# Lightning attention and a gated feed-forward on one core: another order of the work on Pool, Vector and TensorE

## The chip, the cores and the metric

The kernel runs on one core of one Trainium2 chip. The metric is the time of one execution on the device in microseconds (us); four runs of the kernel before gave a median of 242.67 us (241.29 to 244.12). The core's engines are TensorE (PE in the profile; its weight loads are PEld), Vector (DVE), Scalar (ACT), Pool (GpSimd) and Sync (SP). Each takes its own instructions strictly in the order in which the program issues them. Transfers are issued by Pool or by Sync and then carried out by 16 DMA engines.

## The reference

Two stages. The first is linear attention with a decay per head, over batch 4, 8 heads, 768 positions and a head width of 64. The second is a feed-forward with a sigmoid gate on 3072 tokens of width 512, hidden width 1536.

```python
# attention, block by block; lam is one decay per head
intra = einsum('bhic,bhjc->bhij', qb, kb) * Dmask      # Dmask: lam ** (i - j), lower triangle
intra = einsum('bhij,bhjd->bhid', intra, vb)
inter = einsum('bhid,bhde->bhie', qb * lam_pow, kv_state)
out[:, :, sl] = intra + inter
kv_state = lam_block * kv_state + einsum('bhsd,bhse->bhde', kb * rev_pow, vb)
# feed-forward, x is the attention's output with the heads side by side
gate = 1 / (1 + exp(-(x @ w_gate)))
out = (gate * (x @ w_val)) @ w_out
```

## The kernel before

**Tiling.** The kernel uses blocks of 128 positions in place of the reference's 64, so there are six steps n = 0 to 5. In each step it handles 4 batches x 128 positions = 512 tokens. Inputs are cast from float32 to bfloat16 by the loads; products are summed in float32 in PSUM, of which attention has five banks (pool ps_at) and the feed-forward three (ps_ff).

**Pieces.** The work of a step is cut into pieces, each a few lines of code:

- t(n, bp), piece_t: the transposed q of two batches is scaled by the powers of the decay into QS, on Vector (L177, for n > 1, from the tile QR). For n = 0 and 1 TensorE transposes q and k (L160, L169, L184, L190); from n = 2 on transpose_by_dma (L151) makes QR and KR by two transposing transfers on Sync's queue.
- sc(n, bp), m(n, bp): scores of two batches on TensorE (piece_s, L206, two banks for a batch), then the mask product MT, two Vector operations for each batch (piece_m, L214). sc issues the scores of both batches and the masks of the first, m those of the second.
- a(n, bp), piece_a: attention output of two batches on TensorE, from the state Sb (L220) and from MT and v (L227); Scalar copies it to XT (L234), the feed-forward's input.
- make_kd(n): the decayed k, kd, one operation on Pool over 128 x 2048 elements (L238). fade(): the decayed state sd, one Pool operation for each batch (L247).
- c(n, bp), piece_c: the state's update, kd times v on TensorE (L255), added to sd on Vector and written to Sb (L264; for n = 0 a copy, L262).
- gv(n, ft), piece_gv: four gate matmuls (L275), a sigmoid on Scalar (L278), four value matmuls (L281), and on Vector the product ht (L284). Twelve of these make a step. gvh is the same for two batches only (L292 to L302).
- po(n, tt), piece_po: one batch's output projection, twelve matmuls (L307), copied by Scalar (L310) and sent out on Sync's queue (L311).
- load(n, what, b0, b1), L78: q, k or v of a block, issued by Pool. load_gv and load_wo (L84, L85, L89): a slice of the weights, issued by Pool.
- idle(n): matmuls on zeros that keep TensorE busy while block 0 waits for data (L140).

**Order.** Nothing plans the order: it is written by hand, under manual_schedule, and every engine follows the order of the calls. Block 0 (L328 to L351) goes through transposes, scores, masks and attention with idle() between. Pool has by then issued block 0's loads and three slices of weights; make_kd(0), the other slices and the loads of block 1 stand behind them (L314 to L326). Then come the twelve gv of step 0 with the attention of block 1 among them, step 1 with block 1's second half, and from L412 the eight output projections of steps 0 and 1 with block 2's attention between them. The loop from L429 handles steps 2 to 5: in step n, the state's update c(n) after the first two gv, the load of block n + 2, fade and make_kd(n + 2) on Pool, then t, sc, m and a of block n + 1 among gv 2 to 11, and at the end four po in a row. The load of a block and its transposes are issued a step ahead.

Of the kernel before, what the change touches and what calls it, by code (L numbers as in the profile page):

```python
# [8 lines left out]
FP32 = mybir.dt.float32  # L9
# [7 lines left out]
def kernel(  # L17
# [14 lines left out]
    C = 128  # L32
# [49 lines left out]
    def load_gv(i, w):  # L82
        fs = slice(i * w, (i + 1) * w)
        nc.gpsimd.dma_start(out=WG[:, :, fs], in_=wg_r[:, :, fs])  # L84
        nc.gpsimd.dma_start(out=WV[:, :, fs], in_=wv_r[:, :, fs])  # L85
# [12 lines left out]
    nc.vector.memset(ident, 0.0)  # L98
    nc.vector.memset(tri, 0.0)

    load(0, "q", 0, 2)
    load(0, "k", 0, 2)
    for i, base in enumerate((-1, C - 1)):
# [6 lines left out]
                            pattern=[[-1, C]], channel_multiplier=1)  # L110
    load(0, "q", 2, 4)
    load(0, "k", 2, 4)
    load(0, "v", 0, 2)
    load(0, "v", 2, 4)

# [20 lines left out]

    def idle(n, cols=TCH):
        w = ps_ff.tile([128, TCH], FP32, name="wm", tag="ff")
        for i in range(n):
            nc.tensor.matmul(w[:, :cols], lhsT=zero[:, :128], rhs=zero[:, :cols], start=True, stop=True,  # L140
                             skip_group_check=True)
# [13 lines left out]

    def piece_tq0(bp):
        tq = ps_at.tile([128, 2, HP, C], BF16, name="tq", tag="ps")
        for i in range(2):
            for hp in range(HP):
                nc.tensor.transpose(tq[:, i, hp, :], Q[0][:, 2 * bp + i, 2 * hp:2 * hp + 2, :], ident)  # L160
        QS[0, bp] = trsb.tile([128, 2, HP, C], BF16, tag="QS", name="QS")
        nc.vector.tensor_tensor(out=QS[0, bp], in0=tq,
                                in1=lamq.unsqueeze(1).to_broadcast([128, 2, HP, C]), op=ALU.mult)

# [28 lines left out]

    Sb = stp.tile([128, B, HP, 128], BF16, tag="Sb", name="Sb")

    SP, OP = {}, {}

    def piece_s(n, bs):

        for b in bs:  # L200
            bp, i = b // 2, b % 2
            sp = [ps_at.tile([128, HP, C], FP32, name=f"sp{u}", tag="ps") for u in range(2)]
            for hp in range(HP):
                for u in range(2):
                    us = slice(u * 64, (u + 1) * 64)
                    nc.tensor.matmul(sp[u][:, hp, :], lhsT=KS[n, bp][us, i, hp, :],  # L206
                                     rhs=QS[n, bp][us, i, hp, :],
                                     start=(hp == 0), stop=(hp == HP - 1), skip_group_check=True)
            SP[n, b] = sp

    def piece_m(n, b):
# [4 lines left out]
    def piece_a(n, bs):  # L216
# [16 lines left out]
        for b in bs:  # L233
            nc.scalar.copy(XT[n][:, :, b, :], OP[n, b])  # L234

    def make_kd(n):
# [77 lines left out]
    GW = DFF // 6  # L314
    for i in range(3):
        load_gv(i, GW)
    make_kd(0)
# [7 lines left out]
    for i in range(3):  # L325
        load_wo(i, NFT // 3)  # L326

    idle(10)  # L328
    piece_tq0(0)
    idle(4)  # L330
    piece_tk0(0)
    idle(2)
    piece_s(0, [0])
    piece_m(0, 0)
    piece_tq0(1)
    piece_s(0, [1])
    piece_m(0, 1)
    idle(3)
    piece_tk0(1)
    idle(2)  # L340
    piece_s(0, [2])
    piece_m(0, 2)
    piece_s(0, [3])
    piece_m(0, 3)
    nc.vector.memset(Sb, 0.0)
    piece_a(0, [0])
    piece_a(0, [1])
    idle(2)
    piece_a(0, [2])
    piece_a(0, [3])  # L350
    idle(2)  # L351

    def c(n, bp):
        piece_c(n, [2 * bp, 2 * bp + 1])
# [14 lines left out]
    def gv(n, *fts):  # L369
        for ft in fts:  # L370
            piece_gv(n, ft)
# [21 lines left out]
    load(2, "qkv", 0, B)  # L393
    make_kd(2)
    transpose_by_dma(2)
# [7 lines left out]
    gvh(1, 1, 0, 1, 2, 3, 4, 5, 6)  # L403
    gv(1, 7, 8)
    c(1, 0)
    gv(1, 9)
    c(1, 1)
    load(3, "qkv", 0, B)
    fade()
    make_kd(3)  # L410
    gv(1, 10, 11)
    piece_po(0, 0)  # L412
    t(2, 0)
    piece_po(0, 1)
    sc(2, 0)
    m(2, 0)
    t(2, 1)
    piece_po(0, 2)
    sc(2, 1)
    m(2, 1)  # L420
    piece_po(0, 3)
    transpose_by_dma(3)
    piece_po(1, 0)
    a(2, 0)
    piece_po(1, 1)
    a(2, 1)
    piece_po(1, 2)
    piece_po(1, 3)
    for n in range(2, NSTEP):  # L429
        nx = n + 1  # L430
        if nx < NSTEP:
            gv(n, 0)
            c(n, 0)
            gv(n, 1)
            c(n, 1)
            if n + 2 < NSTEP:
                load(n + 2, "qkv", 0, B)
                fade()
                make_kd(n + 2)
            elif nx < NSTEP - 1:  # L440
                fade()
            gv(n, 2)
            t(nx, 0)
            gv(n, 3)
            t(nx, 1)
            gv(n, 4)
            sc(nx, 0)
            gv(n, 5)
            m(nx, 0)
            gv(n, 6, 7)  # L450
            sc(nx, 1)
            gv(n, 8)
            m(nx, 1)
            if n + 2 < NSTEP:
                transpose_by_dma(n + 2)
            a(nx, 0)
            gv(n, 9, 10, 11)
            a(nx, 1)
        else:
            gv(n, *range(NFT))  # L460
        for tt in range(B):
            piece_po(n, tt)

# [29 lines left out]
```

## Time and profile before

| | |
|---|---|
| median of four runs | 242.67 us |
| the profiled execution | 242.25 us |
| its span | 240.1 us |
| TensorE busy | 224.4 us (93%) |
| Vector busy | 114.6 us (48%) |
| Pool busy | 85.6 us (36%) |
| Scalar busy | 80.1 us (33%) |
| mean granted TensorE clock | 0.989 |

The profile shows one execution. Its span runs from the first to the last instruction; the time of the same execution is 2.15 us longer. In a row of the timeline stand the start in us from the span's start, the length, the engine, the line of the kernel, the operation, what it writes <- what it reads, and in brackets the time for which the engine stood before it and what ended that. In a row of the waits stand the waiting engine, its line, what it waited for, then the total in us, how often, and the longest. A row of the windows gives the stretch, its length, and for each engine its busy time and instructions, then the granted clock. A row of the transfers ends with their size and the us from issue to landing; a row of one line's instructions gives the shortest, the median and the longest in ns. A busy time of TensorE holds overlaps, so the length from one start to another is the better measure of what it costs.

### The profile page before, as it was taken

The page shows a single profiled execution, that of the slowest core. Times are in us where ns is not written, and L with a number is a line of the kernel's source. Part 1 is how long each engine was busy: PE and PEld are TensorE (multiplying, and loading weights), DVE is VectorE, ACT ScalarE, POOL GpSimd, SP SyncE. Part 2 cuts the span into 40 slices and gives each one's busy share as a digit, 9 for nine tenths or more (in the row PEclk, how much of TensorE's full clock was granted, in tenths as well). Part 3 has the DMA queues.
Part 4 walks back from the last instruction along what each step waited for, and adds up shares of the span by engine and source line. Part 5 has one row for each costly group of instructions (what it writes and reads, how often), then busy time and mean ns, then how long its engine had stood idle before and what let it go on. Part 6 is the DMA issues. An engine that isn't in the chain of part 4 may idle for free.

```text
span 240.1 us, 3816 instructions
## 1 busy us (share of the span) xinstructions
PE 224.4 (93%) x1528; PEld 115.8 (48%) x1553; DVE 114.6 (48%) x184; ACT 80.1 (33%) x145; POOL 85.6 (36%) x70
## 2 busy tenths in 40 slices
PE   7779999999995999988999997999999999999993
PEld 2444555886542454544554543554544554444441
DVE  2473845744839400799510599620497510243300
ACT  5453244453211033322431332432222431323121
POOL 8999676924976700497000390000000000000000
PEclk9999999999999799999999999999999999999998
DMA  8999999999999999979923750002200002100022
GB/s 54 149 184 194 174 183 168 208 157 155 148 157 221 97 179 146 266 153 98 156 11 130 157 67 0 0 3 87 87 3 1 0 3 99 75 0 0 3 87 87
DMA packets 102289, 24.89 MB, mean 104 GB/s; under 512 B 91520, under 2 KB 99200, under 8 KB 102272
## 3 DMA queue, kind: packets, MB, share of 16 engines
q0 software_dynamic: 82032, 14.16, 80.7%
q1 hardware_dynamic: 20240, 10.49, 20.5%
q8 instruction: 12, 0.20, 0.3%
q14 instruction: 5, 0.04, 0.0%
HBM read 28.32 MB, written 6.29 MB: 144 GB/s over the span
## 4 chain that ended last, share of the span: by engine, by line
PE 87%; DVE 4%; DMA 3%; issue 2%; POOL 2%; ACT 1%; POOLq 0%; DVEq 0%
PE po L307 25%; PE gp L275 24%; PE vp L281 23%; PE sp L206 3%; DMA kb<-in_k_dram 3%; PE vp L298 3%; PE op L227 3%; PE gp L292 2%; PE cp L255 2%; PE op L220 2%; DVE MT L214 2%; DVE QS L177 1%; POOL qb L78 1%; DVE ht L284 1%; POOL kb L78 0%
## 5 line engine op out<-in xcount | busy, mean ns | idle before, releaser
L284 DVE TENSOR_TENSOR ht<-sg,vp 128x512 bf16<-128x512 bf16 x65 | 44.6, 686 | 91.9 <-PE vp L281 90.5
L275 PE MATMUL gp<-XT,WG 128*128 128x512 bf16 x249 | 65.2, 379 | 3.4 <-DVE ht L284 2.4
L281 PE MATMUL vp<-XT,WV 128*128 128x512 bf16 x255 | 66.0, 379 | 0.3
L307 PE MATMUL po<-WO,ht 128*128 128x512 bf16 x281 | 64.2, 383 | 0.4
L278 ACT ACTIVATE sg<-gp 128x512 bf16<-128x512 f32 x65 | 38.8, 597 | 76.4 <-PE gp L275 72.5
L307 PEld LDWEIGHTS <-ht 128*128 128x128 bf16 x288 | 27.9, 99 | 33.7 <-issue 1.3
L281 PEld LDWEIGHTS <-WV 128*128 128x128 bf16 x260 | 25.4, 98 | 30.7
L275 PEld LDWEIGHTS <-WG 128*128 128x128 bf16 x260 | 24.1, 98 | 29.6 <-issue 3.8
L214 DVE TENSOR_TENSOR MT<-sp,mask 128x512 bf16<-128x512 f32 x48 | 30.5, 682 | 7.6 <-PE sp L206 7.6
L310 ACT COPY ob<-po 128x512 f32<-128x512 f32 x24 | 14.1, 586 | 55.0 <-PE po L307 51.2
L247 POOL TENSOR_TENSOR sd<-Sb,dec 128x512 f32<-128x512 bf16 x16 | 16.7, 1071 | 40.4 <-DVE Sb L264 40.4
L238 POOL TENSOR_TENSOR kd<-kb,kds 128x2048 bf16<-128x2048 bf16 x6 | 22.7, 3783 | 13.7 <-PE vp L298 8.0
L234 ACT CAST XT<-op 128x512 bf16<-128x512 f32 x24 | 13.0, 589 | 9.9 <-PE op L227 9.8
L177 DVE TENSOR_TENSOR QS<-QR,lamq 128x1024 bf16<-128x1024 bf16 x8 | 15.5, 1941 | 0.0
L264 DVE TENSOR_TENSOR Sb<-cp,sd 64x256 bf16<-64x256 f32 x32 | 13.5, 421 | 0.8
L78 POOL DMA_DIRECT2D qb<-in_q_dram x8 | 11.9, 1482 | 1.0 <-POOLq L477 0.8
L78 POOL DMA_DIRECT2D kb<-in_k_dram x8 | 11.4, 1426 | 1.1 <-DMA qb<-in_q_dram 1.1
L78 POOL DMA_DIRECT2D vb<-in_v_dram x8 | 11.4, 1427 | 0.6 <-DMA WG<-in_moe_w_gate_dram 0.6
L140 PE MATMUL wm<-zero 128*128 128x512 bf16 x23 | 8.2, 488 | 1.5 <-DVE zero L97 1.2
L302 DVE TENSOR_TENSOR ht<-sg,vp 128x256 bf16<-128x256 bf16 x14 | 5.8, 420 | 6.1 <-PE vp L298 3.8
L206 PE MATMUL sp<-QS,KR 64*128 64x128 bf16 x128 | 5.4, 229 | 3.3 <-DVE QS L177 3.2
L298 PE MATMUL vp<-XT,WV 128*128 128x256 bf16 x56 | 8.4, 272 | 0.1
(51 smaller groups left out, 112.5 us busy)
## 6 DMA issues: line engine op xcount, KB each, us to landing
out_dram<-ob SPq DMA_DIRECT2D x24, 256.0 KB, 2.0
qb<-in_q_dram POOLq DMA_DIRECT2D x4, 512.0 KB, 9.0
kb<-in_k_dram POOLq DMA_DIRECT2D x4, 512.0 KB, 10.9
vb<-in_v_dram POOLq DMA_DIRECT2D x4, 512.0 KB, 14.0
WG<-in_moe_w_gate_dram POOLq DMA_DIRECT2D x6, 256.0 KB, 9.4
WV<-in_moe_w_val_dram POOLq DMA_DIRECT2D x6, 256.0 KB, 9.8
WO<-in_moe_w_out_dram POOLq DMA_DIRECT2D x3, 512.0 KB, 14.2
qb<-in_q_dram POOLq DMA_DIRECT2D x4, 256.0 KB, 7.4
```

The lines of the kernel that those rows point to most:

```text
L78: nc.gpsimd.dma_start(out=t[:, b0:b1], in_=src[b0:b1, :, sl, :].rearrange("b h s d -> s (b h) d"))
L177: nc.vector.tensor_tensor(out=QS[n, bp], in0=QR[n][:, 2 * bp:2 * bp + 2], in1=lamq.unsqueeze(1).to_broadcast([128, 2, HP, C]), op=ALU.mult)
L214: nc.vector.tensor_tensor(out=MT[n, b][:, u], in0=SP[n, b][u], in1=mask[:, u], op=ALU.mult)
L238: nc.gpsimd.tensor_tensor(out=KD[n], in0=K[n], in1=kds.unsqueeze(1).unsqueeze(3).to_broadcast([128, B, H, D]), op=ALU.mult)
L247: nc.gpsimd.tensor_tensor(out=SD[b], in0=Sb[:, b], in1=dec.unsqueeze(2).to_broadcast([128, HP, 128]), op=ALU.mult)
L275: nc.tensor.matmul(gp, lhsT=WG[:, mt, fs], rhs=x[:, mt, :], start=(mt == 0), stop=(mt == NMT - 1))
L278: nc.scalar.activation(sg, gp, AF.Sigmoid)
L281: nc.tensor.matmul(vp, lhsT=WV[:, mt, fs], rhs=x[:, mt, :], start=(mt == 0), stop=(mt == NMT - 1))
L284: nc.vector.tensor_mul(HT[n, ft], sg, vp)
L298: nc.tensor.matmul(vp[:, cs], lhsT=WV[:, mt, fs], rhs=x[:, mt, cs], start=(mt == 0), stop=(mt == NMT - 1))
L307: nc.tensor.matmul(po, lhsT=HT[n, ft][:, tt * 128:(tt + 1) * 128], rhs=WO[:, ft, :], start=(ft == 0), stop=(ft == NFT - 1))
L310: nc.scalar.copy(ob, po)
```

## The change

It moves pieces, and in block 0 splits some. **Steps 1 to 4:** on Pool, fade and make_kd now follow c of the same step directly, make_kd builds the kd that the next step uses (so kd(2) leaves its place ahead of block 2's transposes, and kd(5) is no longer built), and the load of the block after comes behind them. On Sync, a block's transposes are issued at the start of the step before the one that uses it, behind the last outputs. In steps 2 to 4 t(n + 1) stands after the ninth gv, and sc, m and a are spread over the last two gv and the four po. In step 1, c is one gv earlier, three po stand before t(2), and the rest alternates with the other five.

**Block 0:** the memset of Sb goes to the kernel's start. k of batches 2 and 3 is loaded before their q, and the second halves of q and v are loaded batch by batch. The transposes and the scaling of q go by batch. For batches 1 and 2 one of the two mask products is made by Pool from a copy by Scalar (new piece_m2); the scores of batch 2 use two banks of ps_ff. The attention of batch 3 uses two half tiles, copied by Vector and Scalar (new piece_a0). All idle() share one tile. Pool's issues of the second and third slices of weights stand behind its first and second mask product, and make_kd(0) behind those.

```diff
--- before.py
+++ after.py
@@ -97,6 +97,8 @@
     nc.vector.memset(zero, 0.0)
     nc.vector.memset(ident, 0.0)
     nc.vector.memset(tri, 0.0)
+    Sb = stp.tile([128, B, HP, 128], BF16, tag="Sb", name="Sb")
+    nc.vector.memset(Sb, 0.0)
 
     load(0, "q", 0, 2)
     load(0, "k", 0, 2)
@@ -108,10 +110,12 @@
                    allow_small_or_imprecise_dtypes=True)
     nc.gpsimd.affine_select(out=tri, in_=tri, compare_op=ALU.is_gt, fill=1.0, base=0,
                             pattern=[[-1, C]], channel_multiplier=1)
-    load(0, "q", 2, 4)
     load(0, "k", 2, 4)
+    load(0, "q", 2, 3)
+    load(0, "q", 3, 4)
     load(0, "v", 0, 2)
-    load(0, "v", 2, 4)
+    load(0, "v", 2, 3)
+    load(0, "v", 3, 4)
 
     lnl = const.tile([128, H], FP32, tag="lnl")
     nc.scalar.activation(lnl, lam_bc, AF.Ln)
@@ -134,10 +138,11 @@
                             in1=pk.rearrange("p (g u) -> p u g", u=2).unsqueeze(3).to_broadcast([128, 2, HP, C]),
                             op=ALU.mult)
 
-    def idle(n, cols=TCH):
-        w = ps_ff.tile([128, TCH], FP32, name="wm", tag="ff")
+    wm = ps_ff.tile([128, TCH], FP32, name="wm", tag="ff")
+
+    def idle(n):
         for i in range(n):
-            nc.tensor.matmul(w[:, :cols], lhsT=zero[:, :128], rhs=zero[:, :cols], start=True, stop=True,
+            nc.tensor.matmul(wm, lhsT=zero[:, :128], rhs=zero, start=True, stop=True,
                              skip_group_check=True)
 
     QS, KS, MT, XT, KD = {}, {}, {}, {}, {}
@@ -153,14 +158,15 @@
         for bp in range(2):
             KS[n, bp] = kt[:, 2 * bp:2 * bp + 2]
 
-    def piece_tq0(bp):
+    def piece_tq0(bs):
         tq = ps_at.tile([128, 2, HP, C], BF16, name="tq", tag="ps")
-        for i in range(2):
-            for hp in range(HP):
-                nc.tensor.transpose(tq[:, i, hp, :], Q[0][:, 2 * bp + i, 2 * hp:2 * hp + 2, :], ident)
-        QS[0, bp] = trsb.tile([128, 2, HP, C], BF16, tag="QS", name="QS")
-        nc.vector.tensor_tensor(out=QS[0, bp], in0=tq,
-                                in1=lamq.unsqueeze(1).to_broadcast([128, 2, HP, C]), op=ALU.mult)
+        for b in bs:
+            if (0, b // 2) not in QS:
+                QS[0, b // 2] = trsb.tile([128, 2, HP, C], BF16, tag="QS", name="QS")
+            for hp in range(HP):
+                nc.tensor.transpose(tq[:, b % 2, hp, :], Q[0][:, b, 2 * hp:2 * hp + 2, :], ident)
+        for b in bs:
+            nc.vector.tensor_tensor(out=QS[0, b // 2][:, b % 2], in0=tq[:, b % 2], in1=lamq, op=ALU.mult)
 
     def piece_tk0(bp):
         tk = ps_at.tile([128, 2, HP, C], BF16, name="tk", tag="ps")
@@ -191,15 +197,13 @@
         KS[n, bp] = trsb.tile([128, 2, HP, C], BF16, tag="KS", name="KS")
         nc.scalar.copy(KS[n, bp], tk)
 
-    Sb = stp.tile([128, B, HP, 128], BF16, tag="Sb", name="Sb")
-
     SP, OP = {}, {}
 
-    def piece_s(n, bs):
+    def piece_s(n, bs, pool=ps_at, tag="ps"):
 
         for b in bs:
             bp, i = b // 2, b % 2
-            sp = [ps_at.tile([128, HP, C], FP32, name=f"sp{u}", tag="ps") for u in range(2)]
+            sp = [pool.tile([128, HP, C], FP32, name=f"sp{u}", tag=tag) for u in range(2)]
             for hp in range(HP):
                 for u in range(2):
                     us = slice(u * 64, (u + 1) * 64)
@@ -207,6 +211,15 @@
                                      rhs=QS[n, bp][us, i, hp, :],
                                      start=(hp == 0), stop=(hp == HP - 1), skip_group_check=True)
             SP[n, b] = sp
+
+    def piece_m2(n, b, part):
+        if part:
+            nc.vector.tensor_tensor(out=MT[n, b][:, 0], in0=SP[n, b][0], in1=mask[:, 0], op=ALU.mult)
+            return
+        MT[n, b] = mtp.tile([128, 2, HP, C], BF16, tag="MT", name="MT")
+        sc = const.tile([128, HP, C], FP32, tag="sc", bufs=2)
+        nc.scalar.copy(sc, SP[n, b][1])
+        nc.gpsimd.tensor_tensor(out=MT[n, b][:, 1], in0=sc, in1=mask[:, 1], op=ALU.mult)
 
     def piece_m(n, b):
         MT[n, b] = mtp.tile([128, 2, HP, C], BF16, tag="MT", name="MT")
@@ -232,6 +245,17 @@
             XT[n] = xtp.tile([128, NMT, B, C], BF16, tag="XT", name="XT")
         for b in bs:
             nc.scalar.copy(XT[n][:, :, b, :], OP[n, b])
+
+    def piece_a0(b):
+        halves = [ps_at.tile([128, 2, C], FP32, name="op", tag="ps") for g in range(2)]
+        for hp in range(HP):
+            for u in range(2):
+                us = slice(u * 64, (u + 1) * 64)
+                nc.tensor.matmul(halves[hp // 2][us, hp % 2, :], lhsT=V[0][:, b, 2 * hp + u, :],
+                                 rhs=MT[0, b][:, u, hp, :], start=(hp % 2 == 0), stop=(hp % 2 == 1),
+                                 skip_group_check=True)
+        nc.vector.tensor_copy(XT[0][:, 0:2, b, :], halves[0])
+        nc.scalar.copy(XT[0][:, 2:4, b, :], halves[1])
 
     def make_kd(n):
         KD[n] = kdp.tile([128, B, H, D], BF16, tag="kd", name="kd")
@@ -312,8 +336,37 @@
 
 
     GW = DFF // 6
-    for i in range(3):
-        load_gv(i, GW)
+    load_gv(0, GW)
+
+    idle(10)
+    piece_tq0([0, 1])
+    idle(4)
+    piece_tk0(0)
+    idle(2)
+    piece_s(0, [0])
+    piece_m(0, 0)
+    piece_s(0, [1])
+    piece_m2(0, 1, 0)
+    piece_tk0(1)
+    piece_tq0([2])
+    piece_m2(0, 1, 1)
+    load_gv(1, GW)
+    idle(3)
+    piece_tq0([3])
+    piece_s(0, [2], ps_ff, "ff")
+    piece_m2(0, 2, 0)
+    piece_m2(0, 2, 1)
+    load_gv(2, GW)
+    piece_s(0, [3])
+    piece_m(0, 3)
+    idle(3)
+    piece_a(0, [0])
+    piece_a(0, [1])
+    idle(2)
+    piece_a(0, [2])
+    piece_a0(3)
+    idle(2)
+
     make_kd(0)
     load_gv(3, GW)
     load(1, "qk", 0, 2)
@@ -324,31 +377,6 @@
     load(1, "v", 2, 4)
     for i in range(3):
         load_wo(i, NFT // 3)
-
-    idle(10)
-    piece_tq0(0)
-    idle(4)
-    piece_tk0(0)
-    idle(2)
-    piece_s(0, [0])
-    piece_m(0, 0)
-    piece_tq0(1)
-    piece_s(0, [1])
-    piece_m(0, 1)
-    idle(3)
-    piece_tk0(1)
-    idle(2)
-    piece_s(0, [2])
-    piece_m(0, 2)
-    piece_s(0, [3])
-    piece_m(0, 3)
-    nc.vector.memset(Sb, 0.0)
-    piece_a(0, [0])
-    piece_a(0, [1])
-    idle(2)
-    piece_a(0, [2])
-    piece_a(0, [3])
-    idle(2)
 
     def c(n, bp):
         piece_c(n, [2 * bp, 2 * bp + 1])
@@ -391,7 +419,6 @@
     gv(0, 11)
     t(1, 1)
     load(2, "qkv", 0, B)
-    make_kd(2)
     transpose_by_dma(2)
     gvh(1, 0, 0, 1)
     sc(1, 1)
@@ -401,65 +428,62 @@
     a(1, 1)
     gvh(1, 0, 5, 6)
     gvh(1, 1, 0, 1, 2, 3, 4, 5, 6)
-    gv(1, 7, 8)
+    gv(1, 7)
     c(1, 0)
-    gv(1, 9)
+    gv(1, 8)
     c(1, 1)
+    fade()
+    make_kd(2)
     load(3, "qkv", 0, B)
-    fade()
-    make_kd(3)
-    gv(1, 10, 11)
+    gv(1, 9, 10, 11)
     piece_po(0, 0)
+    piece_po(0, 1)
+    piece_po(0, 2)
     t(2, 0)
-    piece_po(0, 1)
+    t(2, 1)
+    piece_po(0, 3)
     sc(2, 0)
     m(2, 0)
-    t(2, 1)
-    piece_po(0, 2)
+    piece_po(1, 0)
     sc(2, 1)
     m(2, 1)
-    piece_po(0, 3)
-    transpose_by_dma(3)
-    piece_po(1, 0)
+    piece_po(1, 1)
     a(2, 0)
-    piece_po(1, 1)
+    piece_po(1, 2)
     a(2, 1)
-    piece_po(1, 2)
     piece_po(1, 3)
     for n in range(2, NSTEP):
         nx = n + 1
-        if nx < NSTEP:
-            gv(n, 0)
-            c(n, 0)
-            gv(n, 1)
-            c(n, 1)
-            if n + 2 < NSTEP:
-                load(n + 2, "qkv", 0, B)
-                fade()
-                make_kd(n + 2)
-            elif nx < NSTEP - 1:
-                fade()
-            gv(n, 2)
-            t(nx, 0)
-            gv(n, 3)
-            t(nx, 1)
-            gv(n, 4)
-            sc(nx, 0)
-            gv(n, 5)
-            m(nx, 0)
-            gv(n, 6, 7)
-            sc(nx, 1)
-            gv(n, 8)
-            m(nx, 1)
-            if n + 2 < NSTEP:
-                transpose_by_dma(n + 2)
-            a(nx, 0)
-            gv(n, 9, 10, 11)
-            a(nx, 1)
-        else:
+        if nx == NSTEP:
             gv(n, *range(NFT))
-        for tt in range(B):
-            piece_po(n, tt)
+            for tt in range(B):
+                piece_po(n, tt)
+            break
+        transpose_by_dma(nx)
+        gv(n, 0)
+        c(n, 0)
+        gv(n, 1)
+        c(n, 1)
+        if nx + 1 < NSTEP:
+            fade()
+            make_kd(nx)
+            load(nx + 1, "qkv", 0, B)
+        gv(n, 2, 3, 4, 5, 6, 7, 8)
+        t(nx, 0)
+        gv(n, 9)
+        t(nx, 1)
+        gv(n, 10)
+        sc(nx, 0)
+        gv(n, 11)
+        m(nx, 0)
+        piece_po(n, 0)
+        sc(nx, 1)
+        m(nx, 1)
+        piece_po(n, 1)
+        a(nx, 0)
+        piece_po(n, 2)
+        a(nx, 1)
+        piece_po(n, 3)
 
 
 # ---- launch: one core; inputs and outputs as the reference has them ----
```

## The prediction

> **What bounds the kernel now.** I read the page first: the span, the granted clock and the shares of the chain that ended last.
>
> ```profile
> span 240.1 us, 3816 instructions
> ...
> PEclk9999999999999799999999999999999999999998
> ...
> PE 87%; DVE 4%; DMA 3%; issue 2%; POOL 2%; ACT 1%; POOLq 0%; DVEq 0%
> ```
>
> TensorE carries 87% of the chain, so only what lets it stand or run slowly can be won, and the clock dips in one slice (about 78 to 84 us). The profiled execution took 242.25 us, 2.15 us more than its span; the sum below is made against it. It lies 0.4 us under the median of the runs, 242.67. Next, the windows, cut where TensorE enters a new stage: blocks 0 and 1; the eight output projections of blocks 0 and 1 with block 2's attention; then one window for each step n = 2, 3, 4, 5.
>
> ```profile
> core 0: us, PE busy (x) PEld busy (x) DVE busy (x) ACT busy (x) POOL busy (x), PEclk, DMA share, GB/s
> 17.57:66.51 48.94, 48.55 (x388) 30.44 (x392) 29.02 (x56) 19.42 (x37) 35.37 (x28) 1.00 1.91 174
> 66.51:95.33 28.82, 25.48 (x175) 12.55 (x177) 10.26 (x11) 6.25 (x11) 12.60 (x8) 0.94 2.12 162
> 95.33:132.30 36.97, 35.44 (x238) 17.56 (x240) 20.41 (x30) 11.66 (x20) 13.16 (x8) 1.00 1.18 134
> 132.30:169.27 36.97, 35.40 (x237) 17.56 (x240) 20.41 (x30) 11.66 (x20) 8.10 (x5) 1.00 0.26 58
> 169.27:204.96 35.69, 35.37 (x238) 17.65 (x241) 17.32 (x30) 11.67 (x20) 0.00 (x0) 1.00 0.08 31
> 204.96:236.08 31.12, 30.93 (x142) 13.91 (x142) 8.26 (x12) 9.52 (x16) 0.00 (x0) 1.00 0.09 34
> ```
>
> The last window is the yardstick: step 5 has no attention, only 144 matmuls of 512 columns, so one costs 31.12/144 = 0.216 us, a gate-and-value pair (gv) 8 x 0.216 = 1.73 and an output projection (po) 12 x 0.216 = 2.59. Steps 2, 3 and 4 do the same TensorE work, yet 2 and 3 take 36.97 and step 4 takes 35.69. Step 4 is the one without Pool work. The window 66.51:95.33 needs 8 x 2.59 = 20.7 for its projections and at most 35.69 - 31.12 = 4.57 for the attention, and takes 28.82. The waits name the two stalls:
>
> ```profile
> PE sp L206 <- DVE QS L177: 3.2, 1, 3.2
> ...
> PE gp L275 <- DVE ht L284: 2.4, 2, 1.2
> ```
>
> The timeline shows where the first comes from:
>
> ```profile
> 63.73 1.78 DVE L264 TENSOR_TENSOR Sb<-cp,sd 64x256 bf16<-64x256 f32 x4
> ...
> 66.51 5.34 PE L307 MATMUL po<-WO,ht 128*128 128x512 bf16 x24
> ...
> 71.79 0.62 PE L206 MATMUL sp<-QS,KR 64*128 64x128 bf16 x16
> ...
> 74.07 3.62 POOL L238 TENSOR_TENSOR kd<-kb,kds 128x2048 bf16<-128x2048 bf16 x1 [3.63 <-DMA kb<-in_k_dram]
> 74.61 3.62 DVE L177 TENSOR_TENSOR QS<-QR,lamq 128x1024 bf16<-128x1024 bf16 x1
> ...
> 78.29 1.03 PE L206 MATMUL sp<-QS,KR 64*128 64x128 bf16 x16 [3.19 <-DVE QS L177]
> ...
> 79.25 6.22 PE L307 MATMUL po<-WO,ht 128*128 128x512 bf16 x24
> ```
>
> Vector's scaling of q (QS) begins inside Pool's decayed k (kd) and ends only 0.54 us after it: 74.07 + 3.62 = 77.69, against 78.23. TensorE stands 3.19 us, and what follows runs slowly: the 16 score matmuls take 1.03 against 0.62, the next 24 projection matmuls 6.22 against 5.34. The second stall, step 2 (step 3 repeats it 36.97 us later), and a QS with Pool empty, from step 4:
>
> ```profile
> 101.35 2.04 POOL L247 TENSOR_TENSOR sd<-Sb,dec 128x512 f32<-128x512 bf16 x2 [0.37 <-DVE Sb L264]
> ...
> 103.35 4.07 POOL L238 TENSOR_TENSOR kd<-kb,kds 128x2048 bf16<-128x2048 bf16 x1
> ...
> 104.46 3.51 DVE L177 TENSOR_TENSOR QS<-QR,lamq 128x1024 bf16<-128x1024 bf16 x1
> ...
> 107.36 1.75 POOL L78 DMA_DIRECT2D qb<-in_q_dram  x1
> ...
> 108.61 1.02 PE L275 MATMUL gp<-XT,WG 128*128 128x512 bf16 x4 [1.21 <-DVE ht L284]
> ```
>
> ```profile
> 176.69 0.68 DVE L177 TENSOR_TENSOR QS<-QR,lamq 128x1024 bf16<-128x1024 bf16 x1
> ```
>
> QS by itself is 0.68 us; behind a kd it is 3.5, the products ht queue behind it on Vector, and the gate matmuls find no free PSUM bank.
>
> **The change, part by part.**
>
> 1. Step 1. The order becomes c(1), then fade and kd(2) and load(3) on Pool, three gv, three po, t(2), a fourth po, scores. Vector's last state sum, now over at 65.5, is over one gv earlier, at 63.8; the last of Pool's faded states follow within a microsecond or so (two take 2.04, a row below), near 65; kd(2) takes 3.62, to 68.7. QS(2,0) waits on Vector only for the last ht and for its transposed q, so it is ready at 67.4, when the last ht is done, and still meets kd(2): it ends near 69.4, the second near 70.1. Nothing stands behind it but score masks, and TensorE asks for the scores only after four po, at 66.51 + 4 x 2.59 = 76.9. Cover 6.8 us; without it the old 3.2 us would return. So the idle time and the slow clock go: 3.19 + (1.03 - 0.62) + (6.22 - 5.34) = **4.48 us**. Counted the other way, the window would need 20.7 and 4.57 less the state matmuls (16 of 128 columns, a quarter of 0.216 each, 0.9), 24.4; 28.82 - 24.4 = 4.4, the same within 0.1.
>
> 2. Steps 2 and 3. Pool's fade and kd(nx) follow c(n) at the head of the step, as they do now, and end some 12 us into it (103.35 + 4.07 - 95.33); the load's three issues (1.75) take it to 17. QS now stands behind the ht of the ninth gv: 9 x 1.73 + 0.9 for c = 16.5, and the product, some 17 us into the step. Both engines have met before and nothing is behind QS. Each step falls to what step 4 costs: 2 x (36.97 - 35.69) = **2.56 us**. The lower bound is TensorE's busy time in step 4, 35.37, as if it had no gap (0.32 more in each of three steps), the upper 36.97, no gain. I take step 4's row, the same work with an empty Pool. New here: the scores and attention stand between po's. After the first score pair TensorE does gv 11 and a po, 4.3 us, before the second needs banks; Vector has four masks (0.68 each) and two ht (0.69) in that time, 4.1 us, and the bank that comes last is freed one mask earlier. Margin about 1 us: hidden, and it is tight in step 1, where one po stands between (2.59 against three masks and a latency).
>
> 3. SP and the loads. load(3) goes behind kd(2), from 60.8 to about 69; load(4) and load(5) behind the next step's fade and kd, some 25 to 30 us later than now. The transposes of block nx are issued behind the last output of step n-1, at the step's start, not a step ahead. Rows for their length, alone and beside a load:
>
> ```profile
> QR<-qb SPq DMA_TRANSPOSE x1, 13.4
> ```
>
> ```profile
> QR<-qb SPq DMA_TRANSPOSE x1, 6.3
> ```
>
> ```profile
> KR<-kb SPq DMA_TRANSPOSE x1, 10.3
> ```
>
> At 6.3, and the second one within 7 us of the first, both have landed 13 us into the step; QS is wanted at 17. At the long rows (second issued 6.9 us after the first, 10.3 to land) 17.2, with the scores wanted at 19. Output transfers come behind them 20 us into the step. Cost nothing, upper bound nothing in those rows; priced as a rival. kd(5), which nothing reads, is gone from Pool.
>
> 4. Block 0. What ends it now, and the transfers that bind it:
>
> ```profile
> 6.99 2.30 POOL L78 DMA_DIRECT2D vb<-in_v_dram  x2
> ...
> 9.26 0.79 POOL L84 DMA_DIRECT2D WG<-in_moe_w_gate_dram  x1
> ...
> 13.97 2.48 DVE L214 TENSOR_TENSOR MT<-sp,mask 128x512 bf16<-128x512 f32 x4 [0.63 <-PE sp L206]
> ...
> 16.19 1.32 ACT L234 CAST XT<-op 128x512 bf16<-128x512 f32 x2 [0.31 <-PE op L227]
> 16.51 0.38 PE L227 MATMUL op<-MT,vb 128*64 128x128 bf16 x7 [0.30 <-DVE MT L214]
> ...
> 16.62 0.91 DVE L345 MEMSET Sb<- 128x1024 uint32 x1 [0.16 <-issue]
> ...
> 17.57 1.02 PE L275 MATMUL gp<-XT,WG 128*128 128x512 bf16 x4
> ...
> 18.43 1.03 PE L281 MATMUL vp<-XT,WV 128*128 128x512 bf16 x4
> ```
>
> ```profile
> WV<-in_moe_w_val_dram POOLq DMA_DIRECT2D x1, 256.0 KB, 8.0
> ```
>
> ```profile
> L247 POOL TENSOR_TENSOR sd<-Sb,dec x16: 1031/1040/1516, 34.5 to 139.3; 128x512 f32<-128x512 bf16 x16
> ```
>
> Removed from Vector: two masks (1.3 us) and the memset of Sb from behind them (0.91, now before the mask that waits for Pool's triangle until 4.78: hidden). Added: Scalar's copies of a score tile (0.66 each by the row of two), Pool's two products, two more issues on Pool. A half load costs 0.79 to 1.15, say 0.88, so two splits add 1.2 us; Pool's own line is then: loads to 10.5, first weights to 12.0, product 13.05, weights 14.55, product 15.6, weights 17.1, kd(0) 20.75, fourth weights. Behind Pool's two waits stand those weights, kd(0) and block 1's loads. The data queue runs behind its issues (the row: value weights issued at 10.01 land at 18.0, 8 us later), and is full through this stretch, so 7 us later for the fourth slice (20.75 and 22.25 against 17.27) costs it at most some tenths. The third batch's attention waits for the product at 15.6, the fourth for v, whose last half lands no sooner than now (15.4); four attentions, two of them with fillers, then two half copies end near 17.4. The first vp cannot start before 18.0, so the gain is at most 0.43. No row has a product of two f32 tiles on Pool; the nearest are sd, 1.03 to 1.52, and kd, 3.62: at 1.52 the product ends 1.0 later, at 3.62 5.1 later, and block 0 with it. I take 1.04, which has the same size and one f32 side: **0.15 us** gained, from 0.43 gained to 5 lost.
>
> The Trainium skill (GPSIMD Engine Reference, section 3.1, Elementwise) gives 4497 ns for a two-input f32 operation of 2048 elements; by an estimate a quarter of it is 1.12 us, and the sum would lose 0.15 us. No run shown here has that form.
>
> Block 1's late k lands just in time and stays so:
>
> ```profile
> 40.57 3.62 POOL L238 TENSOR_TENSOR kd<-kb,kds 128x2048 bf16<-128x2048 bf16 x1 [2.07 <-DMA kb<-in_k_dram]
> ```
>
> ```profile
> 42.46 0.45 PE tk L190 x8
> ```
>
> k is there at 40.57, TensorE wants it at 42.46, less 0.15: 1.7 us of room for a late queue.
>
> Sum: 4.48 + 2.56 + 0.15 = 7.19; 242.25 - 7.19 = 235.06, and part of the 0.4 between this execution and the median makes **235.2 us**.
>
> **The rivals.** *More is won* (12%): the steps with attention reach 35.37 (2 x 1.60 + 0.32 in step 4) and block 0 its 0.43: 4.48 + 3.52 + 0.43 = 8.43, 233.8 us. For it: the 0.32 of gaps in step 4 lie where attention and gv meet, and po may take it better. Against: as many such places as now.
>
> *Block 0 pays* (11%): Pool's products are slow or wait for Scalar. At 1.52 us 236.2, at 3.62 240.3. For it: no such row, and a chain Scalar, Pool, TensorE in place of one Vector operation. Against: it is the size of sd.
>
> *QS is not what holds steps 2 and 3* (9%), or its place is taken by the masks feeding the second scores: the 2.56 stay away, 4.48 + 0.15, 237.6 us. For it: about 1 us of margin. Against: 0.68 for QS beside an empty Pool, and ends that follow kd's end within 0.55 us, three times. By the Trainium skill (SBUF — State Buffer, Who interferes with whom) a Vector instruction with two SBUF inputs and a Pool instruction that reads SBUF exclude each other for a whole instruction, the first one winning; the trace agrees with its 3.6 us, and by it the first half of this rival falls.
>
> *The transposes become the wait* (6%), the other side. They stand at the step's start behind the last output, and steps 2, 3 and 4 each need them. If the second lands W us after the scores want it, 19 us into the step, TensorE stands W in each: 235.2 + 3W, and about 1.3 more each where W nears 3.2, as at 78.29. It is slower than before from W = 2.4, that is, a landing more than 21 us into the step; at W = 3.2 it gives 235.2 + 3 x 4.5 = 248.7. For it: 13.4 us in one row. Against: that row ran beside a load of 512 KB tiles, and now none is under way at a step's start.
>
> **How the numbers follow.** The forecast has 62%, its own range 234.2 to 236.2 from the half microsecond unknown in steps and block 0. From 233.2 (more is won, and some) to 238.0 (steps not won, and the lower part of block 0 pays) some 15% are left out. About 1% is what a measurement of this kernel can tell from none. Faster by over 1%, under 240.2: 62 + 12 + 9 + 8 of block 0's 11 + 1 of the transposes' 6 = 92%. Same: 3 + 2 = 5%. Slower: 3%.
>
> **What would show it.** Right: no wait of PE sp on QS; no dip of the clock after 6 us; steps 2, 3 and 4 equal at 35.3 to 35.8; the projection window at 24.3; in step 1 one QS still long beside kd(2), with nothing waiting; block 0's first gp at 17.2 to 17.6. Wrong: gp later than 18 with Pool's product ahead of it; a PE wait for KR, or for masks at the second scores; k of block 1 landing after 42.

## The result, and the profile after

The changed kernel takes **234.8 us** (median of 12 runs, 234.41 to 236.31), beside 242.79 us for the kernel before (median of 17 runs): the quotient of the medians is 0.967. The ratio on record is 0.976, interval 0.9718 to 0.9801, because it leaves out as slow every run more than 1.5% above the fastest of its kernel, and so, on account of one run at 238.32 us, twelve of the seventeen runs of the kernel before, the profiled one among them. By either figure the changed kernel is faster, by about 2% at the least. The prediction was 235.2 us, range 233.2 to 238.0.

The page of the changed kernel, profiled in an execution of 235.1 us: span, granted clock in 40 slices, and the chain that ended last.

```profile
span 232.8 us, 3830 instructions
...
PEclk9999999999999999999999999999999999999999
...
PE 89%; POOL 4%; DMA 3%; issue 2%; ACT 0%; POOLq 0%
```

The dip of the clock is gone. The same six windows as before, cut at the same matmuls; the columns are those of the prediction's table.

```profile
core 0: us, PE busy (x) PEld busy (x) DVE busy (x) ACT busy (x) POOL busy (x), PEclk, DMA share, GB/s
17.28:66.71 49.43, 48.74 (x388) 30.35 (x393) 28.93 (x56) 19.49 (x38) 35.65 (x30) 1.00 1.88 171
66.71:90.99 24.28, 24.12 (x174) 11.98 (x176) 7.97 (x11) 6.25 (x11) 7.17 (x4) 1.00 1.25 142
90.99:126.53 35.54, 35.13 (x238) 17.57 (x241) 17.54 (x30) 11.66 (x20) 12.70 (x8) 1.00 1.10 104
126.53:162.06 35.53, 35.17 (x237) 17.58 (x240) 17.54 (x30) 11.66 (x20) 12.70 (x8) 1.00 1.05 104
162.06:197.59 35.53, 35.12 (x237) 17.59 (x240) 17.54 (x30) 11.66 (x20) 0.00 (x0) 1.00 0.24 60
197.59:228.87 31.28, 31.09 (x142) 13.97 (x143) 8.26 (x12) 9.52 (x16) 0.00 (x0) 1.00 0.09 34
```

The projections of blocks 0 and 1 fall from 28.82 to 24.28 (4.54 us), steps 2 and 3 from 36.97 to 35.5 each (1.43 and 1.44). Steps 2, 3 and 4 are now equal although Pool has 12.7 us of work in two of them. Everything before the projections grew by 0.2 us, to 66.71 from 66.51 on the span's clock.

One correction to the table of before: in it step 4 took 35.69 and step 5 31.12, with the cut at 204.96. The first matmuls of that gv are on record in the timeline:

```profile
204.80 0.59 PE L275 MATMUL gp<-XT,WG 128*128 128x512 bf16 x2
```

So the cut belongs at 204.80 and step 4 took 35.53 before, as it does now. 204.96 is a row of the chain, which starts a row where the record before it ends (the last projection's, 202.64 + 2.32); the other cuts are starts from the timeline, and there this gv starts 0.16 us earlier.

The timeline of the projections, after: Pool's kd(2), Vector's two scalings of q, and TensorE's first scores.

```profile
65.21 3.62 POOL L262 TENSOR_TENSOR kd<-kb,kds 128x2048 bf16<-128x2048 bf16 x1
...
67.59 2.39 DVE L183 TENSOR_TENSOR QS<-QR,lamq 128x1024 bf16<-128x1024 bf16 x2
68.77 1.76 POOL L78 DMA_DIRECT2D qb<-in_q_dram  x1
...
77.17 0.62 PE L210 MATMUL sp<-QS,KR 64*128 64x128 bf16 x16
...
77.72 2.76 PE L331 MATMUL po<-WO,ht 128*128 128x512 bf16 x12
```

The two still meet once, as forecast. But the scalings are over at 69.98 and the scores come at 77.17, with no wait. In steps 2 to 4 they do not meet; this is the line of the scaling, all eight of them (shortest, median and longest in ns):

```profile
L183 DVE TENSOR_TENSOR QS<-QR,lamq x8: 679/684/1789, 67.6 to 181.1; 128x1024 bf16<-128x1024 bf16 x8
```

The longest, 1.79 us, is the one beside kd(2). It leaves 0.6 of the pair's 2.39 for the second, which ran while Pool was issuing a load (68.77 to 70.53) and was not held by that.

### The profile page after: what moved, and what is told of

Same layout as the page of the kernel before. It is cut to its first block, busy times and chain, and to the rows that moved or that the text cites. A ratio compares the mean times of both kernels' runs of the same rounds, so it can differ in the third digit from the quotient of the medians.

```text
span 232.8 us, 3830 instructions
## 1 busy us (share of the span) xinstructions
PE 222.1 (95%) x1529; PEld 115.2 (49%) x1554; DVE 106.0 (46%) x185; ACT 81.0 (35%) x147; POOL 84.4 (36%) x73
## 4 chain that ended last, share of the span: by engine, by line
PE 89%; POOL 4%; DMA 3%; issue 2%; ACT 0%; POOLq 0%
PE po L331 27%; PE vp L305 24%; PE gp L299 24%; DMA WV<-in_moe_w_val_dram 3%; PE vp L322 3%; PE gp L316 3%; PE sp L210 2%; PE op L240 2%; PE op L233 2%; PE cp L279 2%; POOL vb L78 1%; POOL qb L78 1%; POOL kb L78 1%; PE tk L196 0%; PE tq L190 0%
## 5 line engine op out<-in xcount | busy, mean ns | idle before, releaser
L299 PE MATMUL gp<-XT,WG 128*128 128x512 bf16 x252 | 66.0, 379 | 0.6 <-issue 0.2
L331 PEld LDWEIGHTS <-ht 128*128 128x128 bf16 x288 | 27.1, 98 | 32.2
L227 DVE TENSOR_TENSOR MT<-sp,mask 128x512 bf16<-128x512 f32 x44 | 27.8, 683 | 13.5 <-PE sp L210 13.5
L262 POOL TENSOR_TENSOR kd<-kb,kds 128x2048 bf16<-128x2048 bf16 x5 | 18.1, 3623 | 2.8 <-DMA kb<-in_k_dram 2.8
L247 ACT CAST XT<-op 128x512 bf16<-128x512 f32 x23 | 12.4, 589 | 4.7 <-PE op L240 4.7
L78 POOL DMA_DIRECT2D qb<-in_q_dram x9 | 12.4, 1385 | 0.8 <-POOLq L501 0.8
L78 POOL DMA_DIRECT2D vb<-in_v_dram x9 | 12.2, 1360 | 0.0
L316 PE MATMUL gp<-XT,WG 128*128 128x256 bf16 x56 | 8.4, 273 | 0.0
L240 PE MATMUL op<-MT,vb 128*64 128x128 bf16 x184 | 7.6, 222 | 0.0
```

The source lines that it names most:

```text
L78: nc.gpsimd.dma_start(out=t[:, b0:b1], in_=src[b0:b1, :, sl, :].rearrange("b h s d -> s (b h) d"))
L227: nc.vector.tensor_tensor(out=MT[n, b][:, u], in0=SP[n, b][u], in1=mask[:, u], op=ALU.mult)
L262: nc.gpsimd.tensor_tensor(out=KD[n], in0=K[n], in1=kds.unsqueeze(1).unsqueeze(3).to_broadcast([128, B, H, D]), op=ALU.mult)
L299: nc.tensor.matmul(gp, lhsT=WG[:, mt, fs], rhs=x[:, mt, :], start=(mt == 0), stop=(mt == NMT - 1))
L316: nc.tensor.matmul(gp[:, cs], lhsT=WG[:, mt, fs], rhs=x[:, mt, cs], start=(mt == 0), stop=(mt == NMT - 1))
L331: nc.tensor.matmul(po, lhsT=HT[n, ft][:, tt * 128:(tt + 1) * 128], rhs=WO[:, ft, :], start=(ft == 0), stop=(ft == NFT - 1))
```

## The experiments

Each is a small edit of the kernel before or of the changed one. "Window" is the stretch of the eight projections; spans are of the profiled execution.

**1. Block 0 as before, the rest as changed.** The edit takes the kernel before and puts the changed code behind `gv(0, 0, 1, 2, 3)`.

> Block 0 as before, everything from the first gate matmul on as changed. Theory (the gain is all in the projections of blocks 0 and 1 and in steps 2 and 3, and block 0's new order costs a little because its first value weights land later): first gp at 17.57, first value matmul at 18.43 as before, projections window 24.3, steps 35.5; 0.2 us less than the changed kernel, 234.6 us. Rival (block 0's new order carries part of the gain): slower than the changed kernel, 235.0 or more.

235.02 us (six runs, 234.68 to 235.24), window 24.28, steps 35.53 and 35.53. The stalls' part is confirmed: the new order behind block 0 carries the gain by itself. The part on block 0 missed, and the time lies on the rival's side of 235.0: I had read a loss of 0.2 us from two profiles. In seven profiles with the old block 0 (the kernel before and experiments 1, 3, 4, 5, 6 and 10) the first projection starts at 66.51 to 67.39, mean 66.90; in seven with the new one, two of them with the edits of experiment 9, at 66.28 to 66.92, mean 66.63. Single profiles scatter by more than the difference, and its mean is 0.3 us in favour of the new order.

**2. Block 0 as changed, the steps as before.** The edit is the reverse.

> The changed block 0 with the steps as before. Theory: the two stalls stay, projections window 28.8, steps 2 and 3 at 37.0, span 240.1 + 0.2 = 240.3, about 242.5 us. Rival (block 0 carries part of the gain): span under 239.5.

It missed widely: span 234.5, 236.73 us, where the theory said 242.5. The window and steps 2 and 3:

```profile
66.61:91.21 24.60, 24.35 (x177) 11.97 (x176) 7.17 (x11) 6.24 (x11) 13.71 (x9) 1.00 1.90 168
91.21:126.74 35.53, 35.53 (x241) 17.58 (x240) 17.75 (x30) 11.65 (x20) 12.92 (x8) 1.00 1.68 157
126.74:163.72 36.98, 35.77 (x242) 17.55 (x241) 20.41 (x30) 11.65 (x20) 8.10 (x5) 1.00 0.26 58
```

The old order of steps, yet only step 3 has its stall. The timeline of this kernel where kd(3) and the scaling meet says why:

```profile
74.72 0.68 DVE L183 TENSOR_TENSOR QS<-QR,lamq 128x1024 bf16<-128x1024 bf16 x1
74.98 3.90 POOL L262 TENSOR_TENSOR kd<-kb,kds 128x2048 bf16<-128x2048 bf16 x1 [3.61 <-DMA kb<-in_k_dram]
...
75.46 0.62 PE L210 MATMUL sp<-QS,KR 64*128 64x128 bf16 x16 [0.25 <-DVE QS L183]
```

Pool waits for k of block 3, which landed 0.9 us later than before (74.98 against 74.07), while Vector was 0.1 later (74.72 against 74.61). So Vector came first, ran its 0.68, and kd gave way by 0.28 (3.90 in place of 3.62). In step 2 it is the same, with kd(4) again behind a load:

```profile
100.34 0.68 DVE L183 TENSOR_TENSOR QS<-QR,lamq 128x1024 bf16<-128x1024 bf16 x1
100.71 3.79 POOL L262 TENSOR_TENSOR kd<-kb,kds 128x2048 bf16<-128x2048 bf16 x1 [1.44 <-DMA kb<-in_k_dram]
```

The delay comes through the loads: kd(1) started at 42.14 in place of 40.57, so Pool issued the next loads later (45.70 and 61.74, against 44.13 and 60.82). The kernel before therefore had its 4.5 us stall by a margin of half a microsecond in the landing of one transfer. My theory was right in what stalls and wrong in taking the stall as fixed in the order of the steps. By the number the rival won: block 0's new order alone takes off most of the time, not in block 0 but through the loads that it delays. Timed again, to see whether it holds:

> The changed block 0 with the steps as before, again and timed. Theory (its first profile had QS 0.26 us ahead of kd(3) and the second of step 2 ahead of kd(4), because block 1's and the later loads land about a microsecond later; the order of the two decides): about 236.7 to 238.2 in most runs, with single runs at 242 where the order turns. Rival (block 0's order itself saves time): first gate matmul and projections no different from the changed kernel, so no saving there, and the time would not depend on QS and kd.

237.94 us (six runs, 236.58 to 239.01; ratio 0.9811, 0.9762 to 0.986). The profile has the same order, QS at 74.72 ahead of kd at 75.04. The time falls inside the forecast. The spread of 2.4 us fits an order that turns from run to run in one of the steps, and so does the one run of the kernel before at 238.32 among its 242s, 4.5 below the median; no run with the order turned was profiled, so this is argued, not shown.

**3. The order of two lines.** If the first of the two wins, it must be enough to let Vector ask earlier.

```diff
     sc(2, 0)
-    m(2, 0)
     t(2, 1)
+    m(2, 0)
     piece_po(0, 2)
```

> The kernel before with two lines exchanged: in the projections of blocks 0 and 1 the second scaling of q of block 2 stands ahead of the two masks m(2,0) in place of behind them, so Vector asks for it 1.3 us earlier, near 73.4, before Pool's kd(3) can start near 74.1. Theory (whichever of the two starts first keeps the other out until it has ended): QS about 0.7 us, kd waits a few tenths at most, no wait of 3.2 us and no dip of the clock, projections window 24.3 to 24.8 in place of 28.8; steps 2 and 3 stay at 37.0; about 238.4 us. Rival (Pool has the right of way, or kd needs QS out of its way for another reason): QS still long, window over 28.

238.15 us (four runs, 237.33 to 238.45; ratio 0.9809, 0.9757 to 0.9861), forecast 238.4. Vector is first, and kd takes 3.98; below, the meeting, then the window and step 2:

```profile
74.31 0.68 DVE L177 TENSOR_TENSOR QS<-QR,lamq 128x1024 bf16<-128x1024 bf16 x1
74.48 3.98 POOL L238 TENSOR_TENSOR kd<-kb,kds 128x2048 bf16<-128x2048 bf16 x1 [3.07 <-DMA kb<-in_k_dram]
```

```profile
67.39:91.67 24.28, 24.12 (x174) 11.98 (x176) 7.43 (x11) 6.24 (x11) 13.06 (x8) 1.00 2.07 160
91.67:128.65 36.98, 35.45 (x238) 17.57 (x241) 20.41 (x30) 11.65 (x20) 13.14 (x8) 1.00 1.63 153
```

The window has all of its gain, step 2 none, as it should. The lead was only 0.17 us, not the 0.7 that I had expected, since in this run the scaling came 0.9 us later than expected (the projections start at 67.39, not 66.51) and kd only 0.4.

**4. kd in four operations.** Nothing moves, only the length of what is waited for.

```diff
-        nc.gpsimd.tensor_tensor(
-            out=KD[n], in0=K[n],
-            in1=kds.unsqueeze(1).unsqueeze(3).to_broadcast([128, B, H, D]), op=ALU.mult)
+        for b in range(B):
+            nc.gpsimd.tensor_tensor(
+                out=KD[n][:, b], in0=K[n][:, b],
+                in1=kds.unsqueeze(2).to_broadcast([128, H, D]), op=ALU.mult)
```

> The kernel before with kd made by four Pool operations of one batch each in place of one; nothing moved. Theory (Vector's operation with two SBUF inputs waits until the Pool instruction under way ends, then goes): QS never over 1.7 us, no wait of 3.2 us, no dip of the clock; projections window about 25.2, steps 2 and 3 about 35.9, some 236.5 us. Rival (the two share the memory's rate while both run, or Pool keeps its place through its queue): QS stays near 3.5 us, windows 28.8 and 37.0, 242 us or more.

235.88 us (four runs, 235.5 to 236.27; ratio 0.9725, 0.9673 to 0.9777). The timeline at the first meeting:

```profile
74.13 4.49 POOL L239 TENSOR_TENSOR kd<-kb,kds 128x512 bf16<-128x512 bf16 x4 [2.90 <-DMA kb<-in_k_dram]
74.83 0.89 DVE L177 TENSOR_TENSOR QS<-QR,lamq 128x1024 bf16<-128x1024 bf16 x1
...
75.77 0.62 PE L206 MATMUL sp<-QS,KR 64*128 64x128 bf16 x16 [0.46 <-DVE QS L177]
```

Vector slips in among Pool's four: 0.89 us, not 3.5. It comes inside the first and ends at 75.72; the second, at 75.13, then takes 1.49 us where the others take 1.04. Window 24.81, steps 2 and 3 at 35.53. So it is the Pool instruction under way that is waited for, and no shared rate; by rate, four operations of the same total would have cost the same.

**5. One of Vector's inputs out of SBUF.** The powers of the decay are copied to PSUM as float32, and the scaling reads them there; attention keeps four banks.

```diff
-    ps_at = ctx.enter_context(tc.tile_pool(name="ps_at", bufs=5, space=bass.MemoryType.PSUM))
+    ps_at = ctx.enter_context(tc.tile_pool(name="ps_at", bufs=4, space=bass.MemoryType.PSUM))
...
+    ps_lq = ctx.enter_context(tc.tile_pool(name="ps_lq", bufs=1, space=bass.MemoryType.PSUM))
+    lamp = ps_lq.tile([128, HP, C], FP32, name="lamp", tag="lq")
+    nc.scalar.copy(lamp, lamq)
...
-            nc.vector.tensor_tensor(out=QS[n, bp], in0=QR[n][:, 2 * bp:2 * bp + 2],
-                                    in1=lamq.unsqueeze(1).to_broadcast([128, 2, HP, C]), op=ALU.mult)
+            nc.vector.tensor_tensor(out=QS[n, bp], in0=lamp.unsqueeze(1).to_broadcast([128, 2, HP, C]),
+                                    in1=QR[n][:, 2 * bp:2 * bp + 2], op=ALU.mult)
```

> The kernel before with the powers of the decay for the scaling of q held in PSUM as float32 (one bank taken from attention, which keeps four), so that this Vector operation has one input in SBUF in place of two; nothing moved. Theory (two inputs in SBUF are what makes it meet Pool): QS has one length, about 1.2 us by float32 elements, beside kd and away from it; no wait of 3.2 us; projections window under 25.5. Four banks may cost the steps some tenths. Rival (any Vector operation that reads SBUF beside kd is held): QS near 3.5 us, window 28.8, steps 2 and 3 at 37 or more.

236.41 us in its one run, window 25.13, steps 35.53 and 35.54. The line of the scaling, and the kd that stands beside it:

```profile
L181 DVE TENSOR_TENSOR QS<-lamp,QR x8: 1215/1218/1218, 68.0 to 172.5; 128x1024 bf16<-128x1024 f32 x8
```

```profile
73.97 3.62 POOL L242 TENSOR_TENSOR kd<-kb,kds 128x2048 bf16<-128x2048 bf16 x1 [3.77 <-DMA kb<-in_k_dram]
```

All eight take 1.22 us, to 3 ns, though the scaling at 75.23 lies wholly inside this kd (73.97 to 77.59), and kd keeps its 3.62. The edit changes the type of the input along with its place, so the type could be the cause. The kernel before settles that: there block 1's q is scaled with both inputs in bfloat16 and one of them, tq, in PSUM. That operation lies inside kd(1) (40.57 to 44.19) and is not held, nor is that kd, at 3.62:

```profile
42.72 0.68 DVE L186 TENSOR_TENSOR QS<-tq,lamq 128x1024 bf16<-128x1024 bf16 x1
```

So, in the forms seen here, kd and a Vector operation keep each other out only where the latter has both of its inputs in SBUF. This is the rule of the Trainium skill (SBUF — State Buffer, Who interferes with whom) that the prediction named, and experiments 2 to 5 agree with its two halves: two SBUF inputs, and the first to start.

**6. Fillers in the stall.** Fourteen matmuls on zeros keep TensorE at work while it waits.

```diff
     piece_po(0, 2)
+    idle(14)
     sc(2, 1)
```

> The kernel before with 14 filler matmuls on zeros (3.0 us) ahead of the scores that wait for QS in the projections of block 0 and 1; the wait itself stays. Theory (TensorE's standing 3.2 us brings the half clock that costs 1.29 us of the 4.48): no dip of the clock, score matmuls 0.62 and the next projection 5.3, span 1.3 less, 241.4 us. Rival (the clock drops for another reason, such as the load of the whole chip at that time): dip stays, 242.7 us or more.

241.5 us (ten runs, 240.84 to 241.82; ratio 0.9949, 0.9918 to 0.9979). The wait is still there, its sequel not:

```profile
75.30 3.61 DVE L177 TENSOR_TENSOR QS<-QR,lamq 128x1024 bf16<-128x1024 bf16 x1
...
75.62 3.19 PE L140 MATMUL wm<-zero 128*128 128x512 bf16 x14
...
78.97 0.62 PE L206 MATMUL sp<-QS,KR 64*128 64x128 bf16 x16 [0.16 <-DVE QS L177]
```

The window is 27.53 with the clock at 1.00, against 28.82 at 0.94: 1.29 us, the very 0.41 + 0.88 of the prediction's sum. In the profiled execution it was the idle time, not the load of the moment, that brought the clock down. It need not do so each time. The 40 runs of the kernel before that were timed beside the experiments fall into two groups by their mean granted clock: eight at 0.993 or more take 240.73 to 241.54 us, about what the filled kernel takes, and the rest, at 0.992 or less, take 242.21 or more. It seems that the dip stayed away in the eight; none of them was profiled.

**7. The scaling back to where kd runs**, in the changed kernel, with attention left among the projections.

```diff
-        gv(n, 2, 3, 4, 5, 6, 7, 8)
+        gv(n, 2)
         t(nx, 0)
-        gv(n, 9)
+        gv(n, 3)
         t(nx, 1)
-        gv(n, 10)
+        gv(n, 4, 5, 6, 7, 8, 9, 10)
```

> The changed kernel with the two scalings of q in steps 2 to 4 put back behind the third and fourth gv, where Pool makes kd; scores, masks and attention stay among the last gv and the projections. Theory (the separation in time is what gains): QS near 3 us in steps 2 and 3, a wait of TensorE of some 1.2 us in each, steps 2 and 3 at 36.8, step 4 at 35.5, span 232.8 + 2.5 = 235.3. Rival (what gains is that attention stands among the projections): steps 2, 3 and 4 stay at 35.5, span 232.8.

239.3 us in its one run, span 237.1. Steps 2 and 3 are 37.56, step 4, without kd, 35.53. The direction is as forecast, the size 2.03 a step and not 1.3:

```profile
99.22 4.07 POOL L262 TENSOR_TENSOR kd<-kb,kds 128x2048 bf16<-128x2048 bf16 x1
...
100.33 3.50 DVE L183 TENSOR_TENSOR QS<-QR,lamq 128x1024 bf16<-128x1024 bf16 x1
...
104.48 1.02 PE L299 MATMUL gp<-XT,WG 128*128 128x512 bf16 x4 [1.87 <-DVE ht L308]
```

The wait is 1.87 here and was 1.21. No score matmuls stand in this stretch to fill part of the time in which Vector is held, and a pair of them takes 0.62, nearly the whole difference of 0.66.

**8. Attention back among the gv**, with the scaling still behind kd: t after gv 6 and 7, scores, masks and attention among gv 8 to 11, four projections in a row.

> The changed kernel with scores, masks and attention of steps 2 to 4 all among gv 7 to 11 and the four projections in a row, the scaling of q still behind kd. Theory: steps 2, 3 and 4 at 35.5 to 35.7, span within 0.5 of 232.8. Rival (attention among the projections gains by itself): steps at 36 or more, span over 234.

234.53 us in its one run, span 232.4, steps 35.53, 35.53 and 35.54. In these steps it gains nothing to move the attention among the projections; what gains is that q is scaled when kd is over.

**9. Two looks at block 0**, in the changed kernel. First v of batches 2 and 3 in one load:

```diff
-    load(0, "v", 2, 3)
-    load(0, "v", 3, 4)
+    load(0, "v", 2, 4)
```

> The changed kernel with v of batches 2 and 3 of block 0 in one load. Theory (Pool's two longer issues in front of the first weights make them land at 18.56 in place of 18.0): first value weights land 0.3 to 0.6 earlier, first value matmul at 18.1 to 18.3 in place of 18.62, span 0.3 to 0.5 less. Rival (the data queue is full and its order alone decides): first value matmul stays within 0.1 of 18.62.

First value matmul at 18.61, span 232.8: the rival was right. Pool issued the first weights 0.6 us earlier (9.79 against 10.41) and nothing came of it. Then all masks on Vector, piece_m in place of piece_m2:

> The changed kernel with all eight mask products of block 0 on Vector, so that Pool issues its weights without waiting. Theory (Pool's 1.3 us products in front of the second and third slices and kd(0) make the data queue run dry at the fourth slice, and block 1's late k lands at 42.3 in place of 40.5): it lands at 41.0 or earlier; Vector's two masks more make the first gp come 0.3 to 0.7 later than 17.28; first value matmul unchanged near 18.6, since it waits for weights; span within 0.3 of 232.8. Rival (the products on Pool win block 0's time): first value matmul later than 18.9, span 233.1 or more.

Span 232.7. The first gp came at 17.27, not 0.3 to 0.7 later: as far as one profile can tell, the products on Pool gain block 0 nothing. The first value matmul came at 18.36, and kd(1), which waits for block 1's late k, started at 41.42 against 42.37, not at the 41.0 or earlier of the forecast: Pool's products account for 0.95 of the 1.8 us by which that load had come later (40.57 in the kernel before), and what accounts for the rest is open.

**10. Two small edits together**, those of experiments 3 and 4, on the kernel before.

> The kernel before with kd made batch by batch and the second scaling of q of block 2 ahead of the two masks: two small edits, nothing else moved. Theory (the whole gain is that QS does not stand behind a long kd, however that is reached): projections window 24.3, steps 2 and 3 at 35.5, as in the changed kernel, with the old block 0: 235.0 to 235.4 us, the same as old_block0's 235.0 within what can be measured. Rival (the order of the whole change wins something of its own, by fewer Pool operations or later loads): 0.5 us or more above old_block0.

235.2 us (six runs, 234.81 to 235.55; ratio 0.9686, 0.9654 to 0.9718), window 24.29, steps 35.53 and 35.53, span 232.7. It is the same as the changed kernel in each stage that had a stall; no version here is faster than the changed kernel by more than the runs scatter.

## Why the prediction was right

- **Step 1, 4.48 us: right, measured 4.54.** The scaling still meets kd(2), ends at 69.98 (forecast 70.1), and the scores come at 77.17 (76.9). The split into 3.19 of standing and 1.29 of slow clock is shown by experiment 6. What the step did not see is how near the old stall was to not happening (experiment 2): it let "the old 3.2 us" return as if the order alone decided it, where a landing decided as well.
- **Steps 2 and 3, 2.56 us: mechanism right, size 2.87.** Each fell to step 4's length, as argued; that length was read 0.16 us too long, from the cut at 204.96. The margin of "about 1 us" before the second scores held: TensorE waits for no mask there.
- **Block 0, 0.15 us, "from 0.43 gained to 5 lost": inside the range, with its main price mis-sized.** Between the two profiles the projections start 0.2 us later, over all profiles 0.3 earlier, so the 0.15 can't be told from the scatter. The first gp came at 17.28, inside 17.2 to 17.6; the first value matmul, forecast to start no earlier than 18.0, waited for its weights until 18.62. Pool's product of two float32 tiles, which no row of before showed, is longer than the value taken:

```profile
L222 POOL TENSOR_TENSOR MT<-sc,mask x2: 1324/1336/1347, 11.9 to 14.7; 128x512 bf16<-128x512 f32 x2
```

  1.34 us against 1.04 from sd's row; the estimate by the Trainium skill (GPSIMD Engine Reference, section 3.1, Elementwise), 1.12, is short too. It cost block 0 nothing that shows: with all masks on Vector the first gp comes at the same time (17.27, experiment 9).
- **"Some tenths" for the data queue: too small.** Block 1's late k was there at 42.37 (kd(1) starts on it), 1.8 us later than before, and TensorE reads it at 42.50, without a wait. Of the room, 1.9 us in the kernel before (40.57 to 42.46), 0.13 was left. The prediction's own sign of being wrong, "k of block 1 landing after 42", thus came true without costing time; that nothing came of it was luck, and a little more delay would have made it a wait.
- **The transposes: right.** They start behind the last output at 92.27 and 94.40, take 2.0 and 3.7 us, and nobody waits for them.
- **The sum: in part luck.** It gave 7.19 us against the profiled execution, and the two profiled executions differ by 7.15 (242.25 and 235.1). Of its terms, steps 2 and 3 were 0.31 too small and block 0, in these profiles, 0.35 too large; the two errors cancel.

## What to carry to other kernels

When two engines keep each other out for whole instructions, ask which one starts first and by how much, and make short the instruction that is waited for: half a microsecond of luck decided 4.5 us here, and cutting one Pool operation in four took most of it without moving anything. A mean duration that is several times the shortest of the same shape (1.94 us for QS against 0.68) is the sign to look for on the page. Before trusting a difference of some tenths between two profiles, look at how far profiles of the same code scatter.

## What the runs showed of the hardware that was not expected

- A Vector operation held by Pool ends 0.54 us after Pool's instruction, though alone it takes 0.68 (74.07 + 3.62 = 77.69 and 78.23 in the kernel before). The other way round, kd starts 0.42 us before QS ends and takes only 0.28 longer (experiment 2). In both cases 0.14 us overlap; that a first part of the held operation is done ahead of the hold is a reading of these numbers, not shown.
- TensorE's standing 3.19 us was enough for the lower clock in the profiled execution, which then cost 1.29 us more; 14 matmuls on zeros in that time took away all of it.
- The scaling with one float32 input in PSUM takes 1.22 us in place of 0.68, and the kernel with it is still faster, 236.41 us in its one run, since each long kd no longer holds it.
